# A two-layer Fourier-mixing and gated-unit kernel: another order of its opening, products without a use between the first ones, and tests held away from two loads

## The chip, the core and the metric

The kernel runs as one program on one core of a Trainium2 chip. Its engines are TensorE (PE, with PEld for its weight loads), VectorE (DVE), ScalarE (ACT), GpSimd (POOL) and SyncE (SP), which here issues nearly all transfers (DMAs). All work in SBUF, and PE writes its products into PSUM banks. The metric is the device time of one execution in microseconds (us); a profiled execution also leaves a trace.

## The reference

Two layers work on `x` (2048 rows, 640 columns). Each adds a Fourier transform of the normed rows (over columns, then over rows, real part only), and then a gated unit with 1728 inner columns.

```python
def _A_ref(x, dft_seq_re, dft_seq_im, dft_hid_re, dft_hid_im):
    a = jnp.einsum("bsd,ed->bse", x, dft_hid_re)
    b = jnp.einsum("bsd,ed->bse", x, dft_hid_im)
    return jnp.einsum("ts,bse->bte", dft_seq_re, a) - jnp.einsum("ts,bse->bte", dft_seq_im, b)

def _B_ref(x, w_gate, w_up, w_down):
    g = jnp.einsum("bsd,df->bsf", x, w_gate)
    u = jnp.einsum("bsd,df->bsf", x, w_up)
    return jnp.einsum("bsf,fd->bsd", _sigmoid(g) * u, w_down)

x = x + _A_ref(_layernorm(x), ...)
x = x + _B_ref(_layernorm(x), ...)
x = x + _A_ref(_layernorm(x), ...)
x = x + _B_ref(_layernorm(x), ...)
```

All is float32. The kernel computes with pairs of float16 numbers (a high and a low part), three products for one.

## The kernel before

**What is computed where.** The Fourier matrices are arguments, and the kernel makes use of their symmetry: rows s and 2048 - s are added and subtracted ("folded") before any product, and columns likewise. A fold needs rows in reversed order; PE turns them by a product with a permuted identity. That the matrices really have this symmetry is tested while the kernel runs: 100 tests, each of which loads 128 KB or so of a matrix (lines 1490, 1507, 1550, 1559 on SP), subtracts or adds its parts on DVE (`test_rows`, lines 1497 and 1499, and its like) and sums squares on ACT (line 1469). If a test fails, a general program runs instead (`general`, not run here).

**The opening** (`opening`, line 1593) takes the first layer's transform in an order that is written out by hand: `OPENING` (line 156) is a list of steps, each a word and its indices, and every engine gets its instructions in that order. The rows are in four groups i = 0 to 3 of four tiles A, B, C, D (128 rows, 640 columns, float32). B and C have to be turned:

- `turn i g` is two float32 products on PE of 128x320 (line 352) into one of two PSUM tiles, `twin_124` for B and `twin_125` for C. `turned i g` copies the result out on ACT (line 358) and frees the twin for the next group.
- `stats i g` takes mean and variance of an unturned tile, on DVE (lines 419 and 420) or, for those in `ON_ACT`, on ACT (lines 578 and 579). `square`, `means` and `smeans` do that for turned ones.
- `col i k` folds columns on DVE (lines 588 and 589: two operations of 128x640). `zero i` clears two columns of the folded tile on POOL (line 846).
- `power i` is the root of the variance (line 400 on DVE, then line 401 on POOL), `scale i` the rest of the norm (lines 405 to 409 and 618 on DVE).
- `re`, `ro` (ACT, lines 629 and 631) and `de`, `do` (DVE, line 635) scale and fold rows, and `join i e`, `join i o` (DVE, line 665) join the halves.
- `seq i tp` are then the float32 products over rows (line 824, and 827 for one row kept apart): for group 0 the step `seq 0 0` needs both joins of group 0.
- `evhi`, `ev`, `hid` and later words take the second transform (line 912), the norm of the second half, and the first products of the gated unit.

**After the opening** all work is planned by a schedule in estimated PE time. `steps` lists PE's pieces of work with their lengths; `when(t, f)` puts any other work at time t of that schedule, in front of the piece of PE that stands there. `start_of(layer, "d", h)` is the place where the down projection of half h begins. That projection consists of stages (line 1418 on PE, weights `kept_f` loaded by `load_stage`, line 1366, their result added to the rows on DVE by `rows_add`, line 1292). Before it stand the products of gate and up (`products`, line 1162; their inputs are turned by DMA transposes, line 528) and the `tail` (line 1271), whose weights line 1046 loads.

**Tests in the schedule.** `spans` (line 1958) gives stretches of the schedule with a weight each; the 100 tests are laid over them at a constant pace in weighted time. A test's load stands at its own place, its DVE work two places on.

**Queues.** Each engine works its instructions off in program order. SP does so too: a load that has to wait for its space holds back the loads behind it.

**Places.** SBUF is one tile `big` of 406 units. `Slots` (line 110) gives each piece of it the place that a list of numbers, `PLACES`, names, one after the other; work that takes a place waits for the last reader of what was there.

Of the kernel before, what the change touches and what calls it, by code (L numbers as in the profile page):

```python
# [17 lines left out]
P = 128  # L18
S = 2048
D = 640  # L20
# [3 lines left out]
EH = D // 2  # L24
# [46 lines left out]
JC = 6  # L71
# [35 lines left out]
311 372 252 359 204 297 350 151 264 212 377 100 226 132 161 118 355"""  # L107
# [20 lines left out]
class Slot:  # L128
# [19 lines left out]
GA, GB, GC, GD = range(4)  # L148
# [8 lines left out]
    turn 0 B, wld 4 0, stats 0 A, turned 0 B, turn 0 C, turn 1 B, square 0 B, turned 0 C, stats 0 D, col 0 0,  # L157
    square 0 C, wld 3 0, means 0, col 0 1, smeans 0, turned 1 B, double 0 0, square 1 B, turn 1 C, zero 0, turn 2 B,
    stats 1 D, turned 1 C, double 0 1, square 1 C, power 0, turn 2 C, col 1 0, turned 2 B, stats 1 A, means 1,
    smeans 1, scale 0, double 1 0, stats 2 A, re 0 0, re 0 1, power 1, turned 2 C, ro 0 1, ro 0 0, stats 2 D,  # L160
    col 1 1, square 2 B, turn 3 B, col 2 0, de 0 1, scale 1, square 2 C, de 0 0, do 0 0, col 2 1, row 0, zero 2,
    smeans 2, means 2, turn 3 C, ro 1 0, join 0 e, ro 1 1, double 1 1, re 1 1, do 0 1, do 1 0, power 2, double 2 0,
    re 1 0, join 0 o, turned 3 C, turned 3 B, do 1 1, stats 3 A, square 3 C, zero 1, square 3 B, de 1 1, scale 2,
    de 1 0, join 1 o, seq 0 1, ro 2 0, row 1, stats 3 D, means 3, re 2 0, join 1 e, col 3 1, col 3 0, double 2 1,
    ro 2 1, smeans 3, seq 0 0, de 2 0, re 2 1, power 3, do 2 0, do 2 1, seq 1 1, de 2 1, double 3 0, seq 1 0,
    double 3 1, evhi 0 1 2, ev 0 1 2, wshi 1 0, whhi 1, scale 3, evhi 0 1 1, ro 3 1, join 2 e, join 2 o, wld 4 1,
    re 3 1, evhi 0 1 0, re 3 0, whhi 3, de 3 1, do 3 1, ro 3 0, de 3 0, seq 2 0, do 3 0, whhi 4, join 3 e, join 3 o,
    ev 0 1 1, evhi 0 0 0, wld 5 0, evhi 0 0 2, whhi 2, zero 3, whhi 5, seq 3 0, ev 0 0 0, whlo 5, wshi 3 0,
    evhi 1 0 0, evhi 0 0 1, whhi 0, ev 1 0 0, wld 3 1, seq 2 1, evhi 1 0 1, ev 0 0 2, ev 0 0 1, wshi 2 1, whlo 1,
    whlo 3, whlo 0, whlo 2, wshi 4 1, wshi 1 1, whlo 4, ev 1 0 1, wshi 0 0, hid 0 0, evhi 1 0 2, ev 1 0 2, wslo 1 1,  # L170
    hid 0 1, wslo 2 1, difhi 0, ev 0 1 0, difhi 1, wslo 3 0, dif 0, dif 1, seq 3 1, evhi 1 1 1, hid 1 1, wshi 0 1,
# [8 lines left out]
ON_ACT = {(0, GA), (2, GA), (2, GD), (3, GA), (3, GD)}  # L180
# [22 lines left out]
def folded(ctx, tc, pool, dram, big, acc, flag, x, ct, wh, wg, wu, wc, wd, out):  # L203
# [1509 lines left out]
    def start_of(*key):  # L1713
        return T[marks[key]]
# [427 lines left out]
```

## Time and profile before

| what | value |
|---|---|
| runs of the kernel | 1118.42, 1116.54, 1116.61 us; median 1116.61 us |
| the profiled execution | 1118.15 us, span 1116.3 us (1.85 us lie around the span) |
| mean granted TensorE clock | 0.992 |
| busy: PE, DVE, ACT, POOL | 1090.2, 827.8, 570.8, 157.6 us |
| transfers | 194.70 MB, mean 174 GB/s |

PE is busy for 98% of the span, so what PE waits for is what can be taken out of the time, apart from the clock at which it runs. The span is the time from the first to the last instruction; times in the trace count from the span's start. The second layer's stages of half 0 at 787 to 866 us.

### The profile page before, as it was taken

The page shows a single profiled execution, that of the slowest core. Times are in us where ns is not written, and L with a number is a line of the kernel's source. Part 1 is how long each engine was busy: PE and PEld are TensorE (multiplying, and loading weights), DVE is VectorE, ACT ScalarE, POOL GpSimd, SP SyncE. Part 2 cuts the span into 40 slices and gives each one's busy share as a digit, 9 for nine tenths or more (in the row PEclk, how much of TensorE's full clock was granted, in tenths as well). Part 3 has the DMA queues.
Part 4 walks back from the last instruction along what each step waited for, and adds up shares of the span by engine and source line. Part 5 has one row for each costly group of instructions (what it writes and reads, how often), then busy time and mean ns, then how long its engine had stood idle before and what let it go on. Part 6 is the DMA issues. An engine that isn't in the chain of part 4 may idle for free.

```text
span 1116.3 us, 17439 instructions
## 1 busy us (share of the span) xinstructions
PE 1090.2 (98%) x6279; PEld 620.7 (56%) x6279; DVE 827.8 (74%) x1608; ACT 570.8 (51%) x1108; POOL 157.6 (14%) x245
## 2 busy tenths in 40 slices
PE   5999999999999999999999999999999999999997
PEld 3667444447774444457776844444567444444775
DVE  7986679857548999769786559876797356767962
ACT  7765447765334656455234534575554245454520
POOL 3110143321324143000100100002000010000010
PEclk8899999999999999999999999999999999999999
DMA  8414674365888789656733049635669875665621
GB/s 272 151 37 106 180 208 170 100 214 153 206 232 274 252 228 281 212 171 218 220 90 112 1 88 169 208 120 188 200 150 196 219 228 188 207 207 175 201 84 63
DMA packets 183081, 194.70 MB, mean 174 GB/s; under 512 B 76459, under 2 KB 145476, under 8 KB 182984
## 3 DMA queue, kind: packets, MB, share of 16 engines
q1 hardware_dynamic: 182344, 190.86, 58.4%
q0 software_dynamic: 640, 2.62, 0.6%
q8 instruction: 51, 0.84, 0.3%
q14 instruction: 46, 0.38, 0.1%
HBM read 145.29 MB, written 31.90 MB: 159 GB/s over the span
## 4 chain that ended last, share of the span: by engine, by line
PE 86%; DVE 7%; DMA 5%; ACT 1%; issue 1%; SPq 0%; DVEq 0%; POOL 0%; ACTq 0%; POOLq 0%
PE acc L1162 37%; PE acc L1418 14%; PE acc L1118 14%; PE acc L1304 8%; PE acc L912 4%; DMA big<-in_ct 2%; PE acc L824 2%; PE acc L1399 2%; PE acc L1271 2%; PE acc L781 1%; DMA big<-big 1%; DMA big<-in_x 1%; DVE big L1292 1%; DVE big L239 1%; DVE big L1379 0%
## 5 line engine op out<-in xcount | busy, mean ns | idle before, releaser
L1162 PE MATMUL acc<-big 128*128 128x512 f16 x2160 | 467.8, 379 | 2.8 <-DMA big<-big 1.1
L1162 PEld LDWEIGHTS <-big 128*128 128x128 f16 x2160 | 211.2, 98 | 258.1 <-issue 3.0
L1418 PE MATMUL acc<-big 128*128 128x320 f16 x1512 | 214.0, 299 | 5.1 <-DVE big L1292 2.5
L1418 PEld LDWEIGHTS <-big 128*128 128x128 f16 x1512 | 147.8, 98 | 64.3 <-issue 4.0
L1166 ACT ACTIVATE big<-acc 128x512 f32<-128x512 f32 x160 | 93.8, 592 | 168.6 <-PE acc L1162 168.2
L1118 PE MATMUL acc<-big 128*128 128x512 f16 (+1 forms) x900 | 156.3, 336 | 0.0
L1118 PEld LDWEIGHTS <-big 128*128 128x128 f16 x900 | 87.9, 98 | 67.6 <-issue 0.3
L1469 ACT ACTIVATE big<-big 128x768 f32<-128x768 f32 (+6 forms) x106 | 79.1, 746 | 85.2 <-DVE big L1499 43.9
L239 DVE SCALAR_TENSOR_TENSOR big<-big 128x640 f16<-128x640 f32 (+8 forms) x94 | 75.8, 831 | 22.6 <-POOL big L1072 11.4
L1304 PE MATMUL acc<-big 128*128 128x320 f16 x656 | 89.3, 299 | 0.0
L1292 DVE SCALAR_TENSOR_TENSOR big<-acc,big 128x320 f32<-128x320 f32 x112 | 53.0, 484 | 47.6 <-PE acc L1399 27.3
L1379 DVE TENSOR_TENSOR big<-big 128x512 f16<-128x512 f32 x126 | 84.5, 681 | 4.5 <-ACT big L1378 4.4
L237 ACT ACTIVATE big<-big 128x640 f16<-128x640 f32 (+9 forms) x94 | 63.6, 708 | 43.2 <-DMA big<-in_ct 19.6
L1378 ACT ACTIVATE big<-big 128x512 f16<-128x512 f32 x126 | 72.6, 616 | 18.6 <-DVE big L1379 7.0
L1304 PEld LDWEIGHTS <-big 128*128 128x128 f16 x656 | 64.2, 98 | 25.1
L1212 DVE TENSOR_TENSOR big<-big,acc 128x512 f32<-128x512 f32 x40 | 27.2, 681 | 42.6 <-PE acc L1162 32.0
L1169 ACT ACTIVATE big<-big 128x512 f32<-128x512 f32 x80 | 49.7, 621 | 9.9 <-DVE big L1212 6.8
L381 POOL DMA_INDIRECT out<-big,rows x8 | 9.1, 1140 | 313.0 <-DVE big L1292 168.8
L1497 DVE TENSOR_TENSOR big<-big 128x512 f32<-128x512 f32 x64 | 44.9, 702 | 10.3 <-DMA big<-in_ct 10.1
L511 ACT ACTIVATE big<-big 128x384 f16<-128x384 f32 (+2 forms) x56 | 36.2, 667 | 31.0 <-DVE big L496 18.8
L1390 DVE TENSOR_TENSOR big<-big 128x512 f32<-128x512 f32 x72 | 50.2, 699 | 0.1
L512 DVE TENSOR_TENSOR big<-big 128x384 f16<-128x384 f32 (+2 forms) x56 | 42.6, 774 | 8.4 <-ACT big L511 8.4
(193 smaller groups left out, 1199.1 us busy)
## 6 DMA issues: line engine op xcount, KB each, us to landing
big<-in_ct SPq DMA_DIRECT2D x256, 128.0 KB
big<-kept_f SPq DMA_DIRECT2D x63, 320.0 KB
big<-kept_S SPq DMA_DIRECT2D x33, 512.0 KB
big<-kept_w SPq DMA_DIRECT2D x33, 320.0 KB
big<-in_ct SPq DMA_DIRECT2D x32, 256.0 KB
big<-kept_G SPq DMA_DIRECT2D x21, 320.0 KB
kept_S<-big SPq DMA_DIRECT2D x13, 512.0 KB
big<-in_wg SPq DMA_DIRECT2D x19, 320.0 KB
```

The source lines that it names most:

```text
L237: nc.scalar.activation(dh, src, AF.Copy, scale=s)
L239: nc.vector.scalar_tensor_tensor(dl, src, s, dh, op0=OP.mult, op1=OP.subtract)
L1118: nc.tensor.matmul(ps, w[wp][:, d * P : (d + 1) * P], xt[:, xp, :], start=(d == 0 and wp == HI and xp == HI), stop=(d == ND - 1 and wp == LO))
L1162: nc.tensor.matmul(ps, wt, xt, start=start and n == 0, stop=n == len(todo) - 1, skip_group_check=not start)
L1166: nc.scalar.activation(dst, ps, AF.Copy)
L1292: nc.vector.scalar_tensor_tensor(xe, ps[:, :EH], CB, xe, op0=OP.mult, op1=OP.add)
L1304: nc.tensor.matmul(held["pd", i, e][0][:, :EH], held["t", half, j].parts[hp][:, i * P : (i + 1) * P], held["w", 2, j].parts[wp][:, e * EH ...
L1378: nc.scalar.activation(h, v, AF.Copy)
L1379: nc.vector.tensor_tensor(l, v, h, op=OP.subtract)
L1390: nc.vector.tensor_tensor(o, a, b, op=op)
L1418: nc.tensor.matmul(ps[:, :EH], a[n][hp][:, i * P : (i + 1) * P], w[n][:, wp], start=fresh and m == 0, stop=m == len(todo) - 1, skip_group_ ...
L1469: nc.scalar.activation(v, v, AF.Square, accum_out=new_sum()[:p])
```

## The change

The change has these parts.

1. `OPENING` is another list, and `PLACES` another list of numbers. PE's turnings keep their order.
2. The statistics of tile 0 A go to DVE, those of 0 D to ACT (`ON_ACT`).
3. `zero 0` and `zero 1` come ahead of all columns of their groups.
4. A new word `warm n` makes n products of 128x320 in float32 on PE into a PSUM bank (`acc[3]`), from tile 0 A. Nothing reads them. One stands after `turn 2 C`, two after `turn 3 B`, five after `turn 3 C`.
5. The tests keep away from the second layer's stages of half 0: they end 7 units of the schedule ahead of `start_of(1, "d", 0)`, go on 6 units behind it, and then end 58 units behind it, some 21 ahead of `start_of(1, "j", 1, 0)`, where the next gate and up products begin. The weight in that last stretch goes from 0.4 to 0.45.

```diff
--- before.py
+++ after.py
 PLACES = """
-305 80 399 324 195 319 369 208 352 246 286 400 130 100 81 105 125 153 269 121 156 374 346 273 262 143 116 159
...
+115 380 366 221 234 326 146 85 141 307 80 372 151 90 122 367 401 275 190 272 377 138 258 352 161 108 166 289
...
 OPENING = """
-    turn 0 B, wld 4 0, stats 0 A, turned 0 B, turn 0 C, turn 1 B, square 0 B, turned 0 C, stats 0 D, col 0 0,
-    square 0 C, wld 3 0, means 0, col 0 1, smeans 0, turned 1 B, double 0 0, square 1 B, turn 1 C, zero 0, turn 2 B,
...
+    turn 0 B, turned 0 B, stats 0 A, wld 5 0, turn 0 C, square 0 B, turned 0 C, turn 1 B, zero 0, zero 1, col 0 0,
+    stats 0 D, square 0 C, col 0 1, turn 1 C, turned 1 B, wld 4 0, double 0 1, square 1 B, stats 1 A, stats 1 D,
...
-ON_ACT = {(0, GA), (2, GA), (2, GD), (3, GA), (3, GD)}
+ON_ACT = {(0, GD), (2, GA), (2, GD), (3, GA), (3, GD)}
...
+    def warm(n):
+
+        for _ in range(n):
+            nc.tensor.matmul(acc[3][:, :EH], X[:, GA, :P], X[:, GA, :EH], start=True, stop=True)
...
     spans = [(start_of(0, "d", 0) + 6, start_of(0, "d", 0) + 38, 0.4), (start_of(0, "d", 0) + 76, start_of(0, "e"), 0.55),
-             (start_of(1, "c", 1, 0) + 5, start_of(1, "j", 0, JC), 0.7), (start_of(1, "j", 0, JC), start_of(1, "d", 0), 1.0),
-             (start_of(1, "d", 0), start_of(1, "j", 1, 0), 0.4),
+             (start_of(1, "c", 1, 0) + 5, start_of(1, "j", 0, JC), 0.7), (start_of(1, "j", 0, JC), start_of(1, "d", 0) - 7, 1.0),
+             (start_of(1, "d", 0) + 6, start_of(1, "d", 0) + 58, 0.45),
              (start_of(1, "j", 1, 0), start_of(1, "j", 1, 0) + 50, 0.6),
```

What stands on the engines now is shown at three places. In the new kernel the lines behind `ON_ACT` have numbers that are 5 higher from `warm` on (line 358 is then its product, line 824 becomes 829).

The first is PE from `turn 2 B` on. `twin` are the turnings, `acc` the PSUM banks of all else. Before:

```order
5 L352 MATMUL twin_124<-big 128x320 x2
6 L352 MATMUL twin_125<-big 128x320 x2
7 L352 MATMUL twin_124<-big 128x320 x2
8 L352 MATMUL twin_125<-big 128x320 x2
9 L824 MATMUL acc_64<-big 128x256 x2
10 L824 MATMUL acc_65<-big 128x256 x2
```

The same place in the new kernel:

```order
5 L352 MATMUL twin_124<-big 128x320 x2
6 L352 MATMUL twin_125<-big 128x320 x2
7 L358 MATMUL acc_67<-big 128x320
8 L352 MATMUL twin_124<-big 128x320 x2
9 L358 MATMUL acc_67<-big 128x320 x2
10 L352 MATMUL twin_125<-big 128x320 x2
11 L358 MATMUL acc_67<-big 128x320 x5
12 L829 MATMUL acc_64<-big 128x256 x2
```

Eight products are put between the last turnings and the first `seq`; nothing else moves on PE there.

The second is POOL's start (`rows` are row numbers for later, `quad` the statistics). Before:

```order
10 L248 IOTA rows 128x1 x4
11 L249 IOTA rows 1x1
12 L248 IOTA rows 128x1 x4
13 L249 IOTA rows 1x1
14 L363 TENSOR_SCALAR quad_74<-quad_74 128x3
15 L595 TENSOR_SCALAR big<-big 128x2
16 L846 MEMSET big 128x2
17 L595 TENSOR_SCALAR big<-big 128x2
18 L401 TENSOR_TENSOR quad_74<-quad_74,minus 128x4
```

In the new kernel:

```order
13 L249 IOTA rows 1x1
14 L851 MEMSET big 128x2 x2
15 L600 TENSOR_SCALAR big<-big 128x2
16 L368 TENSOR_SCALAR quad_74<-quad_74 128x3
17 L406 TENSOR_TENSOR quad_74<-quad_74,minus 128x4
```

Both zeros now stand right behind the row numbers, and on DVE the second operation of `col 0 1`, which writes the tile that `zero 0` clears, waits for them. Ahead of `power 0` (line 406, 401 before) DVE now takes `stats 1 A` and `stats 1 D`, which stood behind it.

The third is SP around the second layer's stages of half 0. `kept_f` are the weights of stages, `in_ct` and `in_wh` loads of tests, `kept_w_12` and `kept_w_13` weights for the stages' rest products. Before:

```order
353 L1366 DMA big<-kept_f 128x1280 x3
354 L1550 DMA big<-in_wh 128x1x320 x2
355 L1046 DMA big<-kept_w_12_2350 128x1280
356 L1046 DMA big<-kept_w_13_2364 128x1280
357 L1490 DMA big<-in_ct 128x1x256 x8
358 L1366 DMA big<-kept_f 128x1280 x3
359 L1490 DMA big<-in_ct 128x1x256 x4
360 L1366 DMA big<-kept_f 128x1280 x6
```

In the new kernel:

```order
353 L1371 DMA big<-kept_f 128x1280 x3
354 L1495 DMA big<-in_ct 128x1x256 x4
355 L1051 DMA big<-kept_w_12_2358 128x1280
356 L1051 DMA big<-kept_w_13_2372 128x1280
357 L1495 DMA big<-in_ct 128x1x256 x4
358 L1371 DMA big<-kept_f 128x1280 x9
359 L1555 DMA big<-in_wh 128x1x320 x2
360 L1495 DMA big<-in_ct 128x1x256 x4
```

Between the loads of stage 0 and stage 1 stand two tests instead of three, and none between those of stage 1 and the two that follow.

More of the change, by code (lines that the diff above doesn't have):

```diff
@@ L74 @@
 PLACES = """
[32 rows of a table removed]
-311 372 252 359 204 297 350 151 264 212 377 100 226 132 161 118 355"""
[32 rows of a table added]
+301 372 148 332 160 336 368 276 169 203 280 295 344 208 176 243 225"""
 class Slots:
@@ L156 @@
 OPENING = """
-    turn 0 B, wld 4 0, stats 0 A, turned 0 B, turn 0 C, turn 1 B, square 0 B, turned 0 C, stats 0 D, col 0 0,
-    square 0 C, wld 3 0, means 0, col 0 1, smeans 0, turned 1 B, double 0 0, square 1 B, turn 1 C, zero 0, turn 2 B,
-    stats 1 D, turned 1 C, double 0 1, square 1 C, power 0, turn 2 C, col 1 0, turned 2 B, stats 1 A, means 1,
-    smeans 1, scale 0, double 1 0, stats 2 A, re 0 0, re 0 1, power 1, turned 2 C, ro 0 1, ro 0 0, stats 2 D,
-    col 1 1, square 2 B, turn 3 B, col 2 0, de 0 1, scale 1, square 2 C, de 0 0, do 0 0, col 2 1, row 0, zero 2,
@@ L162 @@
[L162 to L171, printed above, removed]
@@ L172 @@
-    sum 0, wshi 3 1, add 0, nst 1, evhi 1 1 0, ev 1 1 1, nst 0, sum 1, npow 0, add 1, hid 2 0, hidev 2 0, ev 1 1 0,
-    nscale 0, hidev 1 1, cmb 1 1, nrm 0, nst 2, nrm 1, nst 3, npow 1, evhi 1 1 2, hid 3 0, nhi 1, ev 1 1 2, hid 1 0,
-    wslo 0 1, hid 2 1, nlo 1, nscale 1, hidev 3 0, wshi 2 0, wld 5 1, nrm 2, nhi 0, hid 3 1, hidev 2 1, nlo 0,
-    hidev 1 0, nrm 3, nhi 3, tp 0, nhi 2, wslo 1 0, wslo 0 0, tpl 0, nlo 3, wshi 4 0, tp 1, mid, tph 0, nlo 2, tp 3,
-    hidev 3 1, tp 2, cmb 1 0, tph 1, tpl 1, wslo 2 0, jn 1 0, tph 3, midhi, gu 1 0, jn 1 1, tpl 3, middif, tph 2,
@@ new lines @@
+    means 0, smeans 0, power 0, turn 2 B, turned 1 C, square 1 C, turned 2 B, double 0 0, means 1, col 1 0,
+    stats 2 D, col 1 1, smeans 1, turn 2 C, warm 1, scale 0, zero 2, re 0 0, col 2 0, turned 2 C, ro 0 0, power 1, re 0 1,
+    double 1 0, de 0 0, col 2 1, turn 3 B, warm 2, scale 1, square 2 C, ro 0 1, wld 3 0, turn 3 C, warm 5, do 0 1, de 0 1,
+    square 2 B, do 0 0, stats 2 A, double 1 1, ro 1 1, double 2 0, join 0 e, re 1 0, ro 1 0, re 1 1, join 0 o,
+    smeans 2, means 2, do 1 1, turned 3 C, turned 3 B, stats 3 A, do 1 0, zero 3, square 3 C, seq 0 1, square 3 B,
@@ new lines @@
+    power 2, stats 3 D, de 1 0, de 1 1, join 1 o, scale 2, ro 2 0, join 1 e, row 0, double 2 1, col 3 1, means 3,
+    col 3 0, double 3 1, seq 0 0, seq 1 1, re 2 1, ro 2 1, smeans 3, power 3, do 2 0, row 1, seq 1 0, wld 4 1,
+    de 2 1, re 2 0, do 2 1, evhi 0 1 0, evhi 0 1 2, double 3 0, scale 3, de 2 0, ro 3 1, join 2 o, whhi 5, re 3 0,
+    evhi 0 0 2, join 2 e, re 3 1, ro 3 0, de 3 0, evhi 0 1 1, whhi 4, whhi 1, whhi 0, do 3 1, ev 0 0 2, de 3 1,
+    seq 2 0, do 3 0, evhi 0 0 0, join 3 e, evhi 0 0 1, join 3 o, seq 3 0, whhi 2, ev 0 0 0, wld 5 1, whlo 0, whlo 2,
@@ new lines @@
+    ev 0 0 1, whhi 3, whlo 1, whlo 3, whlo 5, evhi 1 0 1, whlo 4, evhi 1 0 0, ev 1 0 0, hid 0 0, wshi 2 1,
+    evhi 1 0 2, ev 1 0 1, wshi 1 0, ev 1 0 2, ev 0 1 1, hid 0 1, ev 0 1 0, ev 0 1 2, difhi 0, seq 2 1, difhi 1,
+    dif 0, dif 1, sum 0, wshi 3 0, add 0, wshi 4 0, nst 1, seq 3 1, nst 0, sum 1, npow 0, add 1, wshi 4 1,
+    evhi 1 1 1, evhi 1 1 0, wld 3 1, wshi 1 1, ev 1 1 1, nscale 0, hid 1 0, nst 2, wshi 0 0, nrm 1, nst 3, hid 1 1,
+    wshi 0 1, evhi 1 1 2, nrm 0, mid, nhi 0, ev 1 1 0, hidev 1 1, npow 1, wshi 2 0, nhi 1, wslo 1 0, ev 1 1 2, nlo 0,
@@ new lines @@
+    wshi 3 1, hidev 1 0, hid 3 0, midhi, nscale 1, tp 0, tpl 0, nlo 1, nrm 3, nhi 3, wslo 1 1, hidev 3 0, hid 2 1,
+    tph 0, middif, nlo 3, wslo 0 0, tp 1, cmb 1 0, tp 3, tph 1, tpl 1, hid 2 0, nrm 2, cmb 1 1, tph 3, hidev 2 0,
+    wslo 0 1, jn 1 0, gu 1 0, nhi 2, nlo 2, tp 2, ad 1 0, tpl 3, tph 2, hid 3 1, jn 1 1, tpl 2, ad 1 1, wslo 4 0,
+    wslo 3 1, pst 2, wslo 4 1, pst 1, gu 1 1, gu 0 0, pst 3, pst 0, wslo 2 0, psc 1, wslo 2 1, ap 2, ap 0, hidev 2 1,
+    hidev 3 1, gu 0 1, ap 3, ap 1, wslo 3 0, pp 1, pp 3, pp 0, gu 2 0, ptr 0, pp 2, ptr 2, ptr 3, gu 2 1, ptr 1"""
@@ L1620, in opening @@
         todo = {
-            "turn": turn_round, "turned": turned, "means": sums_to_means, "square": turned_squares,
+            "turn": turn_round, "warm": warm, "turned": turned, "means": sums_to_means, "square": turned_squares,
             "stats": lambda i, g: (fold_stats_act if (i, g) in ON_ACT else fold_stats)(i, g),
```

2 lines of the change are left out of this document (removed), and 62 rows, old and new, of the table PLACES.

## The prediction

> **What bounds the kernel.** I read the page first, then PE's waits, then the chain of waits and the timelines at the places that the waits name. First the page's span and PE's row.
>
> ```profile
> span 1116.3 us, 17439 instructions
> ...
> PE 1090.2 (98%) x6279; PEld 620.7 (56%) x6279; DVE 827.8 (74%) x1608; ACT 570.8 (51%) x1108; POOL 157.6 (14%) x245
> ```
>
> PE is the bound: 26.1 us of the span are without it. Next, what PE waited for (total, times, longest):
>
> ```profile
> PE twin L352 <- DVE big L308: 4.1, 1, 4.1
> PE acc L824 <- POOL quad L363: 3.6, 1, 3.6
> PE acc L1418 <- DVE big L1292: 2.5, 4, 1.2
> PE acc L1418 <- DMA big<-kept_f: 2.5, 2, 2.3
> ...
> PE acc L1162 <- DMA big<-big: 1.1, 1, 1.1
> ...
> PE acc L824 <- DVE big L665: 0.8, 1, 0.8
> PE acc L1162 <- DVE big L1292: 0.7, 1, 0.7
> ```
>
> The waits of lines 352 and 824 belong to the opening. Those of L1418 and the one of L1162 for a DMA (a transpose, line 528) lie around the second layer's stages of half 0; the timeline of PE shows the former:
>
> ```profile
> 798.82 2.11 PE L1418 MATMUL acc<-big 128*128 128x320 f16 x12 [2.30 <-DMA big<-kept_f]
> 801.10 0.97 PE L1418 MATMUL acc<-big 128*128 128x320 f16 x6 [0.16 <-DMA big<-kept_f]
> ...
> 815.80 2.60 PE L1418 MATMUL acc<-big 128*128 128x320 f16 x18 [1.23 <-DVE big L1292]
> 818.85 3.42 PE L1418 MATMUL acc<-big 128*128 128x320 f16 x24 [0.45 <-DVE big L1292]
> ```
>
> Stage 1 cannot start at 796.5 because its weights are still under way, and some products later DVE is late with the rows of the stage before. The chain of waits from 785 to 822 says why DVE is late: it stood until 794.85 for a test's load of 8.57 us (its line 1497 is a test), and has caught up only with its L1292 at 818.40.
>
> ```profile
> 785.97 8.57 DMA big<-in_ct
> ...
> 794.85 0.70 DVE big L1497
> ...
> 818.40 0.41 DVE big L1292
> ```
>
> SP's timeline shows what the stage's weights stood behind (start, length, issue):
>
> ```profile
> 777.45 1.94 SPq L1550 DMA_DIRECT2D big<-in_wh  x2
> ...
> 783.72 8.92 SPq L1490 DMA_DIRECT2D big<-in_ct  x8
> 792.73 1.52 SPq L1366 DMA_DIRECT2D big<-kept_f  x3
> ...
> 854.38 1.14 SPq L1550 DMA_DIRECT2D big<-in_wh  x2
> ...
> 858.79 9.90 SPq L528 DMA_TRANSPOSE big<-big  x1
> ```
>
> Two tests (eight loads) took SP 8.92 us right ahead of the three `kept_f` loads. The last row is the transpose for which PE waits 1.1 us at 872.
>
> **Part 5, the tests.** Three terms go and one may come.
>
> (a) Between the loads of stage 0 and of stage 1 one hidden-row test (L1550) falls out, and the last test now stands 7 units of the schedule ahead of the stages, where before two stood directly ahead of the `kept_f` loads. Those loads must come 2.30 + 0.16 = 2.5 us sooner. One test is worth 8.92 / 2 = 4.5 us of SP, so the 2.5 us go and about 2 us are left over. Late next would be `rows_add` of stage 0, which is (b). I take -2.5; the ends are -2.5 and 0.
>
> (b) DVE's lateness: the last two tests that are loaded ahead of the gap now have their DVE work behind it, from 6 units after the stages' start on, long after their loads, where before DVE stood for such a load at 794. So the 1.23 + 0.45 = 1.7 us go. They stay if DVE is late for another reason, since the rest of its work there doesn't change: ends -1.7 and 0; I take -1.7, since the chain has a test's load as the start of all the lateness.
>
> (c) The transpose: before, a hidden-row test's loads were issued at 854.38, between the third and the fourth transpose; now they stand ahead of the third. Whether the fourth is quicker for it, I can't read: -1.1 or 0, I take -0.5.
>
> (d) The 100 tests now share less schedule, so they stand 3.3% closer everywhere (a pace of 4.61 units becomes 4.45, worked out from the two lists of spans). Some load or some DVE work may be late where it was just in time. The nearest row is the 0.7 us that a product of L1162 waits for a late L1292; the far end is a wait like the 2.3 us of `kept_f`. I take +0.7, ends 0 and 2.3.
>
> Sum of part 5: -2.5 - 1.7 - 0.5 + 0.7 = -4.0, between -5.3 and +2.3.
>
> **Parts 1 to 4, the opening.** PE's timeline, and the granted clock with it (PE busy in each stretch, then the clock):
>
> ```profile
> 17.51 1.31 PE L352 MATMUL twin<-big 128*128 128x320 f32 x4 [1.11 <-DMA big<-in_x]
> 20.06 2.50 PE L352 MATMUL twin<-big 128*128 128x320 f32 x4 [1.24 <-ACT big L358]
> 26.16 1.19 PE L824 MATMUL acc<-big 128*128 128x256 f32 x2 [3.60 <-POOL quad L363]
> 28.18 10.94 PE L824 MATMUL acc<-big 128*128 128x256 f32 x36 [0.83 <-DVE big L665]
> ```
>
> ```profile
> 13.00:16.50 3.50, 3.07 (x11) 1.61 (x9) 3.06 (x8) 3.47 (x9) 2.46 (x7) 1.00 1.03 383
> 16.50:19.90 3.40, 1.31 (x4) 0.68 (x4) 3.23 (x12) 3.07 (x8) 2.11 (x3) 1.00 1.04 399
> ...
> 26.76:30.17 3.41, 2.58 (x7) 1.62 (x6) 3.26 (x12) 2.83 (x7) 2.39 (x4) 0.50 0.95 267
> 30.17:33.60 3.43, 3.43 (x10) 2.27 (x9) 3.43 (x8) 3.40 (x10) 0.00 (x0) 0.50 1.01 388
> ```
>
> A turning (x4) takes 1.31 us at the full clock and 2.50 at half. The clock fell after the stretch in which PE was busy for 1.31 of 3.40 us, and came back after one in which it was busy throughout, at 33.6; 2.58 of 3.41 didn't bring it back, and 3.07 of 3.50 had kept it. From 28.18 to 33.6 PE works without a pause at half: 5.4 us that would be 2.7 at the full clock.
>
> What sets the start of these products is DVE, with POOL ahead of it:
>
> ```profile
> 12.13 0.37 POOL L248 IOTA rows<- 128x1 int32 x4 [11.04 <-issue]
> ...
> 14.66 1.57 POOL L401 TENSOR_TENSOR quad<-quad,minus 128x4 f32<-128x4 f32 x1 [1.04 <-DVE quad L400]
> ```
>
> ```profile
> 13.41 0.89 DVE L419 BATCH_NORM_STATS2 quad<-big 128x6 f32<-128x320 f32 x2 [0.85 <-DMA big<-in_x]
> ...
> 20.23 0.81 DVE L589 TENSOR_TENSOR big<-big 128x640 f32<-128x640 f32 x1
> ...
> 25.98 1.00 DVE L635 SCALAR_TENSOR_TENSOR big<-big,quad 128x320 f32<-128x320 f32 x2
> ...
> 27.25 0.88 DVE L665 TENSOR_TENSOR big<-big 128x320 f32<-128x320 f32 x2
> ```
>
> (e) POOL does nothing of use before 12.13, and its row numbers end at about 13.0. The zeros come next, so `col 0 1`'s second operation on DVE waits until about 13.0, where before DVE waited until 13.41 for a load. From there to the end of `join 0 o` (27.25 + 0.88 = 28.1) DVE had 14.7 us of work and no wait; now it has one column operation more (0.8) and one row operation fewer (1.00 / 2 = 0.5). 13.0 + 14.7 + 0.3 = 28.0: the same. `join 0 e` now stands right ahead of it and ends at 28.0 - 0.9 = 27.1, 1.0 later than 26.16, which only takes up the pause of 0.83 us behind the first two products. I take -0.2 for the start of the 36. Behind DVE's wait stand the statistics of group 1 and `power 0`, which therefore comes some 1.5 us later than 14.66; POOL's 1.57 us is covered by the four column operations between `power 0` and `scale 0` (4 x 0.8 = 3.2). `scale 0` moves from about 17.9 to 19.9, and with it `re 0 0` on ACT and the copy behind it, which frees the twin:
>
> ```profile
> 19.23 0.68 ACT L358 ACTIVATE big<-twin 128x640 f32<-128x640 f32 x1
> ```
>
> Only one row operation of ACT stands ahead of that copy now, so it ends at about 21.3 instead of 19.9, and `turn 3 C` starts there.
>
> (f) The warm products cost (two make a turning) 0.65 us each at the full clock, 1.25 at half. The three behind `turn 2 C` and `turn 3 B` fill pauses before 21.3. The five behind `turn 3 C` last at the full clock from 22.6 to 25.9, ahead of 27.1: hidden, at no cost. At half they last from 23.8 to 30.1, and the cover is gone: the 36 products start about 2.9 us later than before.
>
> (g) The clock. Stretch 16.5 to 19.9 now has about 2.3 us of PE work (`turn 3 B` and two warm products), 19.9 to 23.35 about 2.0, 23.35 to 26.76 about 2.5. All lie between 1.31 (fell) and 3.07 (kept). If it never falls, 2.7 us go. If it is half for one stretch in which real products run (until 30.2 instead of 33.6), some 1.1 us of the 2.7 stay. I take that one: -1.6. Ends: -2.7, and +1.6 with the half clock until 33.6 and the late start of (f) (3.1 us later, but 3.1 us of work at half less, which is worth 1.5).
>
> (h) Products that come earlier meet joins 1 to 3, for which PE didn't wait. The nearest row is the 0.83 us that it waits for `join 0 o`: I take +0.8, ends 0 and 1.6.
>
> The statistics that change engines, `wld` and the order of `seq 2 1`, `seq 3 1` and `hid` move work of the same size; it lies beside PE's products from 28 us on, where the waits have no row. I cost it at nothing; if ACT or DVE fell behind there it would show as in (h).
>
> Sum of the opening: -0.2 - 1.6 + 0.8 = -1.0, between -2.9 and +3.0.
>
> **Places.** All pieces of `big` have new places, so any load may wait for another reader than before. The rows show that such waits occur on SP (for `kept_w` at line 1046):
>
> ```profile
> SPq L1046 <- PE acc L781: 16.6, 3, 14.8
> ```
>
> None of them reaches PE in the waits above. I take 0; the ends are -1 (the 1.0 or 0.7 us that product rows still wait elsewhere) and +8.
>
> **Sum.** -4.0 - 1.0 = -5.0 against the profiled execution's 1118.15 gives 1113.1; that execution is 1.5 us over the median of the runs, 1116.61, from which -5.0 gives 1111.6. I forecast 1112.
>
> **Rivals.**
>
> 1. The full clock throughout. The waits (a) to (c) go entirely, and PE never falls to half: -5.3 - 2.9 + 0.8 = -7.4, from the median some 1109. For it: PE's busy share never comes as low as the 39% before. Against: three stretches in a row lie nearer to 1.31 than to 3.07 of 3.4, and any of them may be the one at which it falls.
>
> The Trainium skill, page "TensorE: Matmul & The Clock Gate", section "Part 1: The HAM clock gate", has the array throttled again only after a whole idle window of about 3.4 us. By that rule the clock of the new kernel can't fall, and the time is this rival's. The trace of before disagrees with it: the clock fell at 19.9, and the longest pause of PE in the rows ahead of that is 1.11 us.
>
> 2. The tests' gain is eaten. DVE is late at the stages for its own work, not for the test's load, so that (b) and (c) stay, and the closer tests bring a wait like `kept_f`'s elsewhere: -2.5 + 2.3 - 1.0 = -1.2, some 1115.5: no change that can be told. Against: the chain begins with the load.
>
> 3. Slower. A load of weights at the head of SP's queue waits for its new place until a late reader, and everything behind it on SP waits too. It decides when the hold is longer than the slack of the load behind; `kept_f` had none, and 14.8 us is what one such hold lasted. One that reaches PE by 8 us gives -5.0 + 8 = +3, some 1120. For it: every place is new. Against: of the holds that SP has before, the one quoted among them, none comes up in the rows of PE's waits but as `kept_f`'s 2.5. The half clock through the warm products (+3.0) would not do it alone: with -4.0 from the tests it ends at -1.0.
>
> **How the numbers follow.** A measurement of this kernel tells 0.2% (2.2 us) from no change: faster is below 1114.4, slower above 1118.8. The forecast (1110.5 to 1114.4) has a chance of 0.48, rival 1 0.18, rival 2 0.16, rival 3 0.18. So faster 0.68 (the first two and a little of rival 2), same 0.14, slower 0.18. The range has at the bottom the sum of the low ends (-5.3 - 2.9 - 1.0 = -9.2, from the median 1107.4), rounded to 1107, and at the top the price of rival 3, 1120; the likeliest case alone has 1110.5 to 1114.4.
>
> **What would show it.** Right: no row `PE acc L1423 <- DMA big<-kept_f` (line 1418 moves to 1423), and none for a late L1297 there; stage 1 running on from stage 0; in the opening a granted clock of 1.00 from at the latest 30.2 us on, the first of the 36 products at 27.5 to 28.5 us, and L829 ending some 1 to 2 us before its place of before. Wrong: a clock of 0.50 up to 33.6 with the five warm products at 1.25 us; a new wait over 2 us on a load in the rows of PE's waits; or rows of SP that wait long for a place.

## The result, and the profile after

Seven runs of the changed kernel took 1110.53 to 1113.34 us, median 1111.80; seven of the kernel before beside them 1116.54 to 1121.29, median 1118.62. The ratio is 0.9941 with a 95% interval of 0.9927 to 0.9955: 6.6 us faster (5.0 to 8.2). The profiled execution took 1113.34 us (span 1111.5, clock 0.996), 4.8 us less than the one before.

What PE waited for now (total, times, longest):

```profile
PE twin L352 <- DVE big L308: 4.1, 1, 4.1
PE acc L1167 <- ACT big L1171: 3.2, 2, 2.6
PE acc L829 <- issue: 1.9, 1, 1.9
...
PE acc L1167 <- DMA big<-big: 0.6, 1, 0.6
PE acc L1423 <- DVE big L1297: 0.4, 1, 0.4
```

The waits for `kept_f` and for late rows at the stages are gone, and so is the one for the transpose at 872 us. One wait is new: 2.6 us for ACT's L1171 (1166 before, where the waits for it came to 1.0 us). To see where the time went, I compare where the same piece of work starts in the two timelines. First before: the start of the second half's products in layer 1, of the second layer's stages, of a piece after stage 1's wait, of the products behind the stages (which end at 871 us in this profile), and the last such piece.

```profile
338.28 12.03 PE L1162 MATMUL acc<-big 128*128 128x512 f16 x55 [0.70 <-DVE big L1292]
...
786.58 9.94 PE L1418 MATMUL acc<-big 128*128 128x320 f16 x72
...
801.91 0.84 PE L1399 MATMUL acc<-big 128*128 128x320 f16 x5
...
872.27 32.97 PE L1162 MATMUL acc<-big 128*128 128x512 f16 x152 [1.10 <-DMA big<-big]
...
1108.91 0.84 PE L1399 MATMUL acc<-big 128*128 128x320 f16 x5
```

The same places after, with the new wait at 344.87:

```profile
336.30 6.00 PE L1167 MATMUL acc<-big 128*128 128x512 f16 x27 [0.55 <-DMA big<-big]
344.87 5.51 PE L1167 MATMUL acc<-big 128*128 128x512 f16 x18 [2.57 <-ACT big L1171]
...
788.22 12.39 PE L1423 MATMUL acc<-big 128*128 128x320 f16 x90
800.45 0.84 PE L1404 MATMUL acc<-big 128*128 128x320 f16 x5
...
867.55 37.72 PE L1167 MATMUL acc<-big 128*128 128x512 f16 x174
...
1104.18 0.84 PE L1404 MATMUL acc<-big 128*128 128x320 f16 x5
```

| up to | after against before | what happened since the row above |
|---|---|---|
| 336 us | -1.98 us | the opening |
| 788 us | +1.64 us | +3.6: the new wait at 344 us, less 0.6 that is gained at 560 to 575 us |
| 800 us | -1.46 us | -3.1: stage 1 starts without a pause |
| 867 us | -4.72 us | -3.3: late rows and the transpose |
| the end | -4.73 us | nothing |

So the stages gave 6.4 us, the opening 2.0, and the new wait took some 4.2 back. That it took 4.2 and not 2.6 is the clock. In this profile it changes at 344.45 and 347.86 us, so it is half for 3.41 us. Stretches of this length around it (PE busy, then after the four other engines' busy times the clock):

```profile
341.03:344.45 3.42, 1.27 (x6) 0.49 (x5) 1.12 (x1) 1.12 (x2) 1.88 (x3) 1.00 0.92 324
344.45:347.86 3.41, 2.99 (x8) 1.04 (x8) 3.38 (x7) 2.90 (x5) 1.52 (x2) 0.50 0.55 189
347.86:351.27 3.41, 3.41 (x17) 1.55 (x16) 3.34 (x8) 0.86 (x2) 0.00 (x0) 1.00 0.85 281
```

In 2.99 busy us of the half stretch PE made 8 products, and 17 in the 3.41 us behind it. One pause of 2.57 us brought a whole stretch at half clock behind it, which costs another 1.6 us.

The pause starts on SP. Its timeline after shows a test's four loads ahead of the three `in_wd` loads (lines 1333 to 1336), which before stood ahead of the test (1328 to 1331 there):

```profile
327.68 6.90 SPq L533 DMA_TRANSPOSE big<-big  x1
334.62 2.61 SPq L1495 DMA_DIRECT2D big<-in_ct  x4
337.28 0.46 SPq L1335 DMA_DIRECT2D big<-in_wd  x1
```

ACT stands 4.88 us for them with a split of weights (L237), and behind that in its queue is the L1171 that copies PE's bank out and frees it:

```profile
343.33 1.00 ACT L237 ACTIVATE big<-big 128x960 f16<-128x960 f32 x1 [4.88 <-DMA big<-in_wd]
344.24 0.58 ACT L1171 ACTIVATE big<-acc 128x512 f32<-128x512 f32 x1
```

DVE shows why the rows are in time now. Before, its last long stand for a test's load ended 3.7 us behind the stages' start (786.58); after, the stand is no shorter, but it ends 8.6 us ahead of that start (788.22). The two stands, before and after:

```profile
790.30 0.49 DVE L1554 TENSOR_TENSOR big<-big 128x320 f32<-128x320 f32 x1 [4.85 <-DMA big<-in_ct]
```

```profile
779.58 0.49 DVE L1559 TENSOR_TENSOR big<-big 128x320 f32<-128x320 f32 x1 [5.34 <-DMA big<-in_wh]
```

On SP, the weights of stages 1 to 3 are now issued from 0.5 us ahead of the stages' start, where those of stage 1 came 6.2 us behind it (792.73):

```profile
784.05 3.45 SPq L1495 DMA_DIRECT2D big<-in_ct  x4
787.75 9.88 SPq L1371 DMA_DIRECT2D big<-kept_f  x9
```

The opening after, on PE, and in stretches of 3.41 us at whose ends the clock changes (at 27.01 and 30.42 us in this profile, so they don't lie where those of before lay):

```profile
20.30 1.34 PE L352 MATMUL twin<-big 128*128 128x320 f32 x4 [0.67 <-ACT big L363]
21.48 2.86 PE L358 MATMUL acc<-big 128*128 128x320 f32 x10
26.24 10.77 PE L829 MATMUL acc<-big 128*128 128x256 f32 x38 [1.91 <-issue]
```

```profile
16.77:20.18 3.41, 2.39 (x8) 1.44 (x8) 3.27 (x10) 2.54 (x8) 1.22 (x3) 1.00 1.04 397
20.18:23.59 3.41, 3.29 (x12) 2.39 (x13) 3.27 (x11) 3.41 (x9) 3.00 (x6) 1.00 0.83 216
23.59:27.01 3.42, 1.44 (x6) 0.50 (x4) 3.42 (x13) 3.39 (x9) 0.66 (x4) 1.00 0.90 229
27.01:30.42 3.41, 3.41 (x8) 2.49 (x9) 3.31 (x12) 3.38 (x9) 1.90 (x3) 0.50 0.95 309
```

The warm products end at 24.3 and hide ahead of the first sum at 26.24. In the opening the clock falls once, behind the stretch that is busy for 1.44 of 3.42 us, and is back at 30.42.

### The profile page after: what moved, and what is told of

It reads as the page before. It is cut to its first block, busy times and chain, and to the rows that moved or that the text cites. A ratio compares the mean times of both kernels' runs of the same rounds, so it can differ in the third digit from the quotient of the medians.

```text
span 1111.5 us, 17471 instructions
## 1 busy us (share of the span) xinstructions
PE 1091.5 (98%) x6295; PEld 621.8 (56%) x6295; DVE 828.8 (75%) x1608; ACT 570.9 (51%) x1108; POOL 152.1 (14%) x245
## 4 chain that ended last, share of the span: by engine, by line
PE 83%; DVE 6%; DMA 5%; SPq 3%; ACT 1%; issue 1%; POOL 1%; DVEq 0%; POOLq 0%; ACTq 0%
PE acc L1167 38%; PE acc L1423 17%; PE acc L1123 14%; PE acc L917 4%; PE acc L1404 3%; PE acc L1276 2%; DMA big<-in_wu 2%; PE acc L829 2%; PE acc L786 1%; SPq L533 1%; SPq L1495 1%; DMA big<-in_wd 1%; DVE big L239 1%; DMA big<-in_x 1%; DMA big<-in_ct 1%
## 5 line engine op out<-in xcount | busy, mean ns | idle before, releaser
L1171 ACT ACTIVATE big<-acc 128x512 f32<-128x512 f32 x160 | 94.0, 592 | 181.7 <-PE acc L1167 169.8
L239 DVE SCALAR_TENSOR_TENSOR big<-big 128x640 f16<-128x640 f32 (+7 forms) x94 | 75.7, 829 | 19.1 <-ACT big L237 19.0
L237 ACT ACTIVATE big<-big 128x640 f16<-128x640 f32 (+9 forms) x94 | 63.8, 707 | 48.9 <-DMA big<-in_ct 21.9
L1395 DVE TENSOR_TENSOR big<-big 128x512 f32<-128x512 f32 x72 | 50.2, 699 | 0.1
L917 PE MATMUL acc<-big 128*128 128x321 f16 (+3 forms) x324 | 48.6, 300 | 0.0
```

The costliest lines, as they stand in the source:

```text
L237: nc.scalar.activation(dh, src, AF.Copy, scale=s)
L239: nc.vector.scalar_tensor_tensor(dl, src, s, dh, op0=OP.mult, op1=OP.subtract)
L917: nc.tensor.matmul(ps[:m, :EC], z[:, at : at + m], w[:, 384 * wp : 384 * wp + EC], start=(d == 0 and zp == HI and wp == HI), stop=(d == ND ...
L1171: nc.scalar.activation(dst, ps, AF.Copy)
```

## The experiments

Each is compared with runs of the kernel before on the same chip. None of them leaves out anything of the computation.

**e1: the tests' new places alone, in the kernel before.** Places in SBUF stay, but for the two that are now asked for in another order.

```diff
-             (start_of(1, "c", 1, 0) + 5, start_of(1, "j", 0, JC), 0.7), (start_of(1, "j", 0, JC), start_of(1, "d", 0), 1.0),
-             (start_of(1, "d", 0), start_of(1, "j", 1, 0), 0.4),
+             (start_of(1, "c", 1, 0) + 5, start_of(1, "j", 0, JC), 0.7), (start_of(1, "j", 0, JC), start_of(1, "d", 0) - 7, 1.0),
+             (start_of(1, "d", 0) + 6, start_of(1, "d", 0) + 58, 0.45),
```

> The kernel before with the new spans of the tests alone. Theory A (the ledger of the two traces): the tests' new places take 6.4 us out of the stretch from 560 to 872 us, and the same closer pace puts a test's loads ahead of the loads of line 1330 at 338 us, which costs 4.2 us (2.6 of waiting and 1.6 of half clock behind it): about 2 us faster than before, with a wait of PE for ACT at 340 to 350 us. Rival B: the wait at 344 us comes from the new places in SBUF or the new opening, not from the pace: 6 to 6.5 us faster than before, and no such wait.

Measured 1115.16 us (1112.50 to 1115.64) against 1118.15, ratio 0.9961 (0.9945 to 0.9978): 4.4 us faster (2.5 to 6.2). Theory A's 2 lies below that interval, and its upper part takes in rival B's 6, so the time doesn't tell the two apart. The wait that does is there, in a kernel whose opening and places are the old ones:

```profile
346.81 5.52 PE L1162 MATMUL acc<-big 128*128 128x512 f16 x17 [2.62 <-ACT big L1166]
```

So the tests' new places make it, without the new opening, and the waits at the stages go with the tests alone. Why the median gains more than 2 us isn't shown; this profile, with 1115.56 us, is 2.6 below that of before.

**e2: all of the change but the tests' places** (the spans of before in the changed kernel).

> The changed kernel with the old spans of the tests. Theory A: only the opening's gain is left, 1.8 us faster than before, no wait of PE over 1 us at 344 us, and the waits for kept_f at 797 and for late rows at 815 are back. Rival B (the wait at 344 us comes from places or opening): 1.8 - 4.2, so 2.4 us slower than before.

Measured 1116.10 us (1113.88 to 1119.69), ratio 0.9977 (0.9964 to 0.9989): 2.6 us faster (1.2 to 4.0). The wait at 344 us is absent; those at the stages are back, the longest under another name: it ends with DVE's L1247, and the loads of `kept_f` come in just behind it:

```profile
795.55 0.99 PE L1423 MATMUL acc<-big 128*128 128x320 f16 x6 [2.25 <-DVE big L1247]
796.85 0.99 PE L1423 MATMUL acc<-big 128*128 128x320 f16 x6 [0.31 <-DMA big<-kept_f]
...
812.32 2.60 PE L1423 MATMUL acc<-big 128*128 128x320 f16 x18 [0.86 <-DVE big L1297]
815.38 6.82 PE L1423 MATMUL acc<-big 128*128 128x320 f16 x49 [0.45 <-DVE big L1297]
```

Theory A has e2's time and, in both, the waits that come and go; it doesn't have e1's time. 4.4 and 2.6 add up to 7.0, near the change's 6.6.

**e3: the changed kernel without its eight products of no use.**

```diff
-    ... turn 2 C, warm 1, scale 0, ... turn 3 B, warm 2, scale 1, ... turn 3 C, warm 5, do 0 1, ...
+    ... turn 2 C, scale 0, ... turn 3 B, scale 1, ... turn 3 C, do 0 1, ...
```

> The changed kernel without its eight products that nothing reads. Theory A (the clock falls after a stretch of 3.4 us in which PE is busy for well under three quarters): the clock falls at 19.9 or 23.3 us, the first products of the sums run at half until 30 to 34 us, and the time is 0.5 to 1.7 us over that of the changed kernel. Rival B (it takes a whole idle stretch of 3.4 us): the clock stays full, and the time is that of the changed kernel. Rival C (the products of no use only delay what follows): up to 1 us faster.

Measured 1113.40 us (1111.30 to 1118.59), ratio 0.9953 (0.9940 to 0.9967) against the changed kernel's 0.9941: the intervals overlap, and this comparison decides nothing. The clock behaves as A says: at half from 20.22 us on, behind a stretch busy for 1.50 of 3.41 us, without any idle stretch of 3.4 us. Yet it is back at 30.46 here and at 30.42 there, since the sums' own products fill the stretch from 27.0, so that in these two profiles the real products ran at half for the same 3.4 us.

**e4: the one test's load behind the three `in_wd` loads**, in the changed kernel. `forms` is the place of those loads; a test's load (its four transfers) that falls less than 3 units ahead of it is put just behind it.

```diff
-        when(at_test(n), within, n % 3, load, *key)
+        t, forms = at_test(n), start_of(0, "j", 1, 0) - 12
+        when(forms + 0.1 if forms - 3 < t < forms else t, within, n % 3, load, *key)
```

> The changed kernel with one test's load put behind the three loads of line 1333, 1335 and 1336 that it stands ahead of at 334 us; all else as it was. Theory A: the wait of 2.6 us at 344 us goes, and with it the half clock behind it: 4 us faster than the changed kernel, about 1108. Rival B: the loads come late for their own size or for the transposes ahead of them, and the wait stays within 0.5 us: no change.

Measured 1108.43 us (1107.59 to 1110.83), ratio 0.9912 (0.9896 to 0.9929): 9.8 us faster than before, and better than either kernel; against the changed kernel's gain of 6.6 that is 3.2 more. ACT now waits 0.73 us instead of 4.88, and PE runs on without the pause:

```profile
337.48 1.00 ACT L237 ACTIVATE big<-big 128x960 f16<-128x960 f32 x1 [0.73 <-DMA big<-in_wd]
```

```profile
334.59 15.71 PE L1167 MATMUL acc<-big 128*128 128x512 f16 x72 [0.28 <-DMA big<-big]
```

Theory A is shown: the loads of one test in the wrong place cost 3 to 4 us, where the opening's change had brought 2.0 in the profiles and 2.6 in e2's runs.

**e5: e4 once more**, as the reference of the next three.

> The kernel of e4 once more, beside the next three. Theory A: about 1108.4 as before; its runs fall where the clock either has a stretch at half in the first products of the sums or has none, some 1 to 2 us apart.

Measured 1108.71 us (1107.37 to 1109.92), ratio 0.9913 (0.9890 to 0.9936). The gain of e4 repeats on another chip. In four of its six runs the granted clock was 0.999, in two 0.997; the latter took 1109.64 and 1109.92 us, the others 1107.37 to 1108.92. That fits theory A. e4's six runs, of the same kernel, fit it only in part: the fastest of them, the profiled one with 1107.59, has 0.997. Its trace says why: the half stretch lay at 14.41 to 17.83 us, where PE made turnings and had none of the sums' products yet (the rows stand in the last section). So the mean clock alone doesn't price a half stretch; it matters what runs in it.

**e6: e5 without the products of no use.**

> e5 without the eight products of no use. Theory A (they shorten the time at half clock, in some executions to nothing): 0.5 to 1.7 us over e5, its clock at half from about 21 to 30 us in the profile. Rival B (they bring nothing, since the half stretch from 26.8 to 30.2 us stays in either): within 0.4 us of e5. The profiles of the changed kernel and of e3 speak for B (the sums' products began -1.77 and -1.82 us against before), the medians of their runs, on different chips, for A (1.6 us).

Measured 1110.08 us (1108.86 to 1111.48), ratio 0.9930 (0.9907 to 0.9952): 1.4 us over e5, with six runs each that overlap. The clock separates them better than the time: 0.993 to 0.996 in all six runs of e6, 0.997 to 0.999 in e5. With the products of no use 7 of the 12 executions of e4 and e5 have 0.999 and the others 0.997, without them none of e6's six is above 0.996. So they shorten the time at half clock, and in somewhat more than half of the executions to nothing, which the single profiles of the changed kernel and of e3 could not tell, since the half stretch happened to be there in both. Theory A, but on the time at the edge of what the runs can tell.

**e7: eight such products behind `turn 3 C` instead of five.**

> e5 with eight instead of five products of no use behind turn 3 C, so that the pause of 1.5 to 1.9 us ahead of the first sum is nearly filled. Theory A (the stretch from 23.4 to 26.8 us is what lets the clock fall, being busy for 1.4 to 1.9 of 3.4 us): the clock stays full in the profile from 16 us on, 0.5 to 1.2 us faster than e5. Rival B (the clock falls all the same, for the pauses between the turnings): at half the three more cost up to 3 x 0.54 to 3 x 1.1 us: 0 to 2 us slower than e5.

Measured 1109.30 us (1108.36 to 1109.90), ratio 0.9921 (0.9898 to 0.9943): no gain over e5 that can be told. Theory A is right on the clock, as the stretch ahead of the sums is now filled and nothing falls:

```profile
23.35:26.76 3.41, 3.10 (x12) 1.69 (x10) 3.41 (x12) 3.38 (x9) 0.75 (x4) 1.00 0.79 213
```

and wrong on the time. Two things take the gain away. Four of e5's six runs have the full clock already and nothing to win. And the profiles show a loss at the other end: at 336 us e7 is 1.4 us ahead of e5's profile (334.64 against 336.00), but at 1081 us PE waits for late rows, which neither e4's nor e5's profile has. DVE had stood for the reduction of the tests' results on POOL (L1582), 6.47 us here against 4.43 in e5 and 4.66 in e4:

```profile
1078.82 0.15 DVE L1585 TENSOR_SCALAR small<-fin 128x1 f32<-128x1 f32 x1 [6.47 <-POOL fin L1582]
```

```profile
1081.16 2.60 PE L1423 MATMUL acc<-big 128*128 128x320 f16 x18 [0.71 <-DVE big L1297]
```

That is one profile; whether all of e7's runs have this wait isn't known.

**e8: `zero 0` and `zero 1` behind `col 0 1`, as before**, in e5.

> e5 with zero 0 and zero 1 behind col 0 1, as before, so that DVE doesn't stand for POOL. Theory A: DVE's wait of 1.1 to 1.25 us at 10.2 us goes and all of DVE's work up to the joins of group 0 comes 0.6 to 1.2 us sooner: as much faster than e5. Rival B: DVE then stands for the load of tile 1 A until about 11.5 to 12.5 us, and nothing is gained: within 0.4 us of e5.

Measured 1108.79 us (1106.18 to 1110.62), ratio 0.9914 (0.9890 to 0.9938): as e5. DVE's wait for POOL is gone and the first sum starts at 25.25 us instead of 25.98, but the median doesn't show 0.7 us. So part 3 of the change, the early zeros, can't be told from none by these runs; it stays open.

**e9: e4 with tests up to the stages' start**, and from it on.

```diff
-    ... (start_of(1, "j", 0, JC), start_of(1, "d", 0) - 7, 1.0), (start_of(1, "d", 0) + 6, start_of(1, "d", 0) + 58, 0.45),
+    ... (start_of(1, "j", 0, JC), start_of(1, "d", 0), 1.0), (start_of(1, "d", 0), start_of(1, "d", 0) + 58, 0.45),
```

> The kernel of e4 with tests allowed up to the start of the second layer's stages of half 0, and right behind it; the end at 58 units stays. Theory A (the test loads in front of stage 1's weights were what made both kept_f and DVE late): the waits for kept_f at about 793 us (2 to 3 us) and for late rows at 808 us (1 to 2 us) are back, 3 to 5 us slower than e4, about 1112; no wait at 862 us. Rival B (the waits of before came from the places or from the old pace): within 1 us of e4.

Measured 1117.05 us (1115.46 to 1119.03), ratio 0.9992 (0.9982 to 1.0001): nothing is left of e4's 9.8 us, where theory A had 3 to 5 lost. The waits that A names are back:

```profile
796.65 2.62 PE L1423 MATMUL acc<-big 128*128 128x320 f16 x18 [1.41 <-DMA big<-kept_f]
...
814.63 5.64 PE L1423 MATMUL acc<-big 128*128 128x320 f16 x28 [2.79 <-DVE big L1297]
```

The second again brings a stretch at half clock, behind one in which PE was busy for 0.65 of 3.41 us:

```profile
811.87:815.28 3.41, 0.65 (x5) 0.48 (x5) 3.34 (x7) 3.41 (x8) 0.00 (x0) 1.00 0.76 249
815.28:818.69 3.41, 3.41 (x15) 1.96 (x13) 3.34 (x7) 0.71 (x3) 0.00 (x0) 0.50 0.87 249
```

That is 4.2 us of waits and some 1.5 of clock. The gap also sets the pace of all tests, so e9 changes more than one thing, but the profiles of e9 and e4 tell the parts from each other. The second half's products in layer 1 start at 334.60 and 334.59 us, so the opening is the same. The second layer's stages start at 785.29 and 782.33: 3.0 us are lost ahead of them, by the other pace (waits for ACT's L1171 come to 1.6 us against 0.3 in e4, and two for late rows at 559 and 569 us to 1.7 against 0.4). The products behind the stages start at 870.90 and 861.65: 6.3 us of the 9.3 between the two profiles are lost at the stages. Theory A's mechanism holds; its price of 3 to 5 was too low.

**e10: e4 with tests up to the products behind the stages**, the gap at their start kept.

```diff
-             (start_of(1, "d", 0) + 6, start_of(1, "d", 0) + 58, 0.45),
+             (start_of(1, "d", 0) + 6, start_of(1, "j", 1, 0), 0.45),
```

> The kernel of e4 with tests up to the products at start_of(1, j, 1, 0), instead of an end 21 units ahead of them; the gap at the stages' start stays. Theory A (the fourth transpose is late for a hidden-row test's loads ahead of it): a wait of 0.6 to 1.5 us for a transpose at 862 us is back, 1 us slower than e4; no wait at 793 us. Rival B (the transpose was late since DVE was): no wait there, within 0.5 us of e4.

Measured 1116.57 us (1114.17 to 1120.54), ratio 0.9986 (0.9972 to 1.0000). The wait for the transpose is back with 1.33 us, as theory A has it (a hidden-row test stands ahead of the fourth transpose again), and none at 793 us:

```profile
813.05 2.60 PE L1423 MATMUL acc<-big 128*128 128x320 f16 x18 [0.90 <-DVE big L1297]
...
869.75 10.52 PE L1167 MATMUL acc<-big 128*128 128x512 f16 x48 [1.33 <-DMA big<-big]
```

The issue of that transpose takes SP 10.72 us here and 9.90 before, each with a hidden-row test's loads right ahead of it, and 6.35 in the changed kernel without. The first row shows that late rows are back too, with 0.90 and then 0.45 us, though the gap is kept: at the other pace DVE stands for a test's load until 784.51, only 2.8 us ahead of the stages' start (787.26).

But the kernel lost 8 us and not 1. Against e4's profile 2.1 us are lost up to 336 us, 2.8 from there to the stages' start and 3.2 behind it. The first part holds a half stretch at 27.7 to 31.1 us, on the sums' products, where e4's lay on turnings; the second, like e9's, comes with the other pace, among others as a wait with the name of the one at 344 us:

```profile
445.57 4.69 PE L1167 MATMUL acc<-big 128*128 128x512 f16 x21 [1.25 <-ACT big L1171]
```

Its cause is another, though: ACT stood 3.95 us for DVE (L1261), which had a test's work of 3.0 us (L1502 and L1504) ahead of that.

**e11: e7 and e8 together.**

> e8 with eight products of no use behind turn 3 C, so e4 with both small gains of the opening's profiles (e7's full clock, e8's earlier joins). Theory A: the first sum's products begin 3.5 to 4 us ahead of before's, and the time is 1107 to 1108. Rival B: a pause filled moves nothing that the median can tell: 1108 to 1109.5.

Measured 1109.22 us (1107.94 to 1111.35), ratio 0.9921 (0.9906 to 0.9937): rival B. Its profile has the wait of e7's at 1082 us, with 1.45 us, behind a stand of DVE of 7.21 us for POOL. Of the versions tried, e4 (e5) stays the best, at 1108.4 and 1108.7 us.

## Why the prediction came out right

The forecast was 1112 us in a range of 1107 to 1120; 1111.8 was measured. The waits that were to go did go, and by the tests' places, as e1, e2 and e9 show. That the number came so close is luck. The sum has -5.0, and the two profiles give -4.8, but by parts the stages gave 6.4 instead of 4.7 us and the opening 2.0 instead of 1.0, and the closer tests cost 3.6 instead of 0.7. These misses of 1.7, 1.0 and 2.9 cancel. The forecast also set out from the median of three runs, 1116.61; the seven runs of before have 1118.62, and against them the gain is 6.6 us (5.0 to 8.2), with the forecast's 5.0 at its lower edge.

- (a) `kept_f`: -2.5 forecast, -3.1 found between 788 and 801 us. e1, e2 and e9 show that the tests' places alone take this wait away and bring it back (in e2 with DVE's L1247 as the last that PE waits for). One test's loads still stand directly ahead of stage 1's on SP; the gap of 7 units moves them in time and not out of the queue. Counted from the stages' start, the weights are issued 6.6 us sooner, where the prediction counted 4.5.
- (b), (c) late rows and the transpose: -1.7 and -0.5 forecast, -3.3 found together. The transpose's wait went entirely, and e10 brings it back with a hidden-row test ahead of it; the prediction took half of it. Its reading of DVE needs a correction: DVE did not stand until 794.85, where its L1497 starts without a pause. It stood for a test's load until 790.30 and worked on from there with pauses of at most 0.69 us, too late for the stages. Such a stand is still there in the changed kernel, earlier. Three profiles fit that: with a stand that ends 8.6 us ahead of the stages (the changed kernel) no rows are late, with one that ends 2.8 ahead (e10) or 3.7 behind (before) they are.
- (d) the closer tests: +0.7 forecast with a far end of 2.3; found +4.2 at 344 us, less 0.6 of waits that went. This is the term that failed. One of the prediction's own signs of being wrong, a new wait over 2 us on a load, came with it, in a row that names ACT and not the load that ACT stood for. The mechanism was named right (a load late where it was just in time), but the price was bounded by waits that PE already had; the row to look at was the order of SP's loads at each place where a test stands close to a load that another engine waits for. And the bound left the clock out: a pause of 2.57 us costs 4.2.
- (e) the start of the sums: -0.2 forecast, -1.2 found for the 36 products (27.0 against 28.18). POOL's row numbers began at 10.90 us and not at 12.13, so DVE stood until 11.79, not 13.0. From there my count held: 14.7 + 0.3 us of DVE's work would end at 26.8, and the joins ended at 26.94. The earlier start of POOL was not forecast and has no explanation here, so this gain of 1 us is luck as well:

```profile
11.79 0.84 DVE L594 TENSOR_TENSOR big<-big 128x640 f32<-128x640 f32 x1 [1.10 <-POOL big L851]
...
25.26 1.68 DVE L670 TENSOR_TENSOR big<-big 128x321 f32<-128x321 f32 x4
```

- (f) the warm products: hidden, as forecast. But the five behind `turn 3 C` ended at 24.3 and not at 25.9, since that turning began at 20.30 instead of 21.3 and they took 2.86 / 5 = 0.57 us each instead of 0.65. That left a pause of 1.91 us ahead of the first sum.
- (g) the clock: one stretch at half for real products, as chosen, but not by the path that was worked out. The stretch ahead of the sums was to be busy for about 2.5 us; it had 1.44, for the pause of (f). A stretch of 2.5 would have kept the clock in every profile here, and a row of the profile before could have told: a stretch there with 1.76 us kept it (794.76 to 798.17, shown below), so the bound lay between 1.31 and 1.76 and not up to 3.07. PE's lead over before grew from 1.2 us at the first of the 36 products to 2.1 at 37 us, so the clock gave 0.9 where -1.6 was forecast. In the profiles of e4 and e7 no product of the sums runs at half.
- (h) waits for joins 1 to 3: +0.8 forecast, no such wait found. The lead does shrink from 2.1 to 1.5 us up to 60 us and is 2.0 at 336; what makes these steps isn't shown.
- Places: 0 forecast. No wait was found that they made; behind the opening e2, with all the new places, has none over 1 us but those at the stages. No run has the new places alone, though.

Of the rivals, the second, that DVE is late for its own work alone, is ruled out by e1, where the tests' places alone make the rows come in time. The full clock (0.999) is what two of the changed kernel's seven runs show (1110.53 and 1111.02 us) and four of six of e5, so it is in part a matter of the execution: in e4's and e5's profiles, of one kernel, the clock first rises at 7.59 and at 9.29 us, and the stretches lie differently against the work. The third rival, a load at the head of SP's queue that waits for its new place, didn't occur. What it has in common with the wait at 344 us is that loads in front held back what others needed; there a test's four loads did, by the 2.61 us that SP took to issue them, and the price was 4.2 us.

## What to carry to other kernels

Work that may stand anywhere, such as tests, is not free when its loads share one queue with loads that others wait for: keep it away from the places where a load has no slack, and after any change of its pace look through the order of that queue, since one test's loads in the wrong place took back more than half of what the move had brought (4.2 of 6.4 us). A pause of PE costs more than its length when the clock falls behind it (4.2 us for one of 2.57), so price pauses together with the granted clock of the stretch that follows.

## What the runs showed of the hardware

The clock goes by stretches of 3.4 us: while there was work, its half periods lasted 3.41 us (the changed kernel), 10.24 (e1, e3, e6) and 13.65 (before, from 19.93 to 33.59), which is one, three and four times as long. In stretches counted from these changes, it fell where PE had been busy for 0.65 (e9), 0.82 (e1), 1.27 (the changed kernel at 344 us), 1.31 (before) and, as the most, 1.58 us (e9's opening) of 3.41. It stayed up behind 1.76 (before), 1.84 (e1) and 1.88 (e4). So in these profiles the bound lies between 1.58 and 1.76 of 3.41 us, about half. No stretch behind which it fell while products were still to come was idle throughout, and the pauses in them were 2.8 us at most. The Trainium skill, page "TensorE: Matmul & The Clock Gate", section "Part 1: The HAM clock gate", has it fall after a whole idle window of about 3.4 us; the length of the stretch agrees, that it has to be idle does not. The row nearest above the bound, from the profile before, and three from e4's:

```profile
794.76:798.17 3.41, 1.76 (x13) 1.04 (x11) 3.31 (x8) 1.67 (x3) 0.00 (x0) 1.00 0.85 285
```

```profile
11.00:14.41 3.41, 1.50 (x5) 0.68 (x4) 2.56 (x6) 3.35 (x10) 1.40 (x10) 1.00 1.05 304
14.41:17.83 3.42, 3.34 (x7) 2.17 (x8) 3.35 (x8) 1.54 (x5) 2.59 (x3) 0.50 1.03 389
24.65:28.07 3.42, 1.88 (x8) 1.03 (x7) 3.42 (x9) 3.42 (x9) 0.58 (x2) 1.00 0.86 253
```

POOL's row numbers began at 12.12 and 12.13 us in the two profiles with the old opening, and at 9.79 to 10.90 in the eleven with the new one, each time after 8.7 to 11.0 us of idle time for which the profile names no releaser. What sets that start stays open.
